# Two weight-split subtractions per step moved to VectorE in the first block, and the weight decode's low bits moved to ScalarE

## The chip, the cores and the metric

The kernel runs on one core of one Trainium2 chip. The metric is the device time of one execution in microseconds. A program starts each execution by itself; several executions of one kernel give a median.

Five engines work side by side, each on its own queue in order: TensorE (PE in the profile, its weight loads PEld), VectorE (DVE), ScalarE (ACT), GpSimd (POOL) and SyncE (SP), which here only starts transfers. Instructions on different engines wait for each other through semaphores.

## What is computed

An attention layer over chunks of 32 tokens with 8 memory keys, then a feed-forward layer, then a soft mixture of eight experts. Cut to what matters here:

```
x   = attention(q, k, v, mem_k, mem_v)      # 3072 tokens x 512
h   = x @ w_in                              # 512 -> 2048
g   = s * relu(h)**2 + b
x   = g @ w_out                             # 2048 -> 512
out = soft_moe(x, phi, w1, w2)
```

`w_in` and `w_out` arrive in device memory as 64-bit floats (the factor they are scaled with makes them so), 16 slices of 1,024 columns on 128 partitions.

## The kernel before, in words

**Blocks and steps.** The 3,072 tokens are 6 blocks of 512 (`NB`), and the feed-forward width is 16 slices of 128 (`NF`). One step `n` is one slice of one block: 96 steps in all. A step multiplies the block's `x` by the slice's `w_in` (`mm_h`, L269), makes `g` of the result (`make_g`, L275 to L278), and one step later multiplies `g` by the slice's `w_out` (`mm_y`, L289), which adds up in four PSUM banks. The steps of block 0 are n = 0 to 15; they are called the first block here.

**Three products for one.** Each operand is split into a high part, rounded to the fast matmul format, and a low part, the remainder. High times high, high times low and low times high are added, so a step has 12 matmuls in `mm_h` and 12 in `mm_y`. The split of the weights is made anew in every step: `split_wi` (L256 on ScalarE rounds, L257 on GpSimd subtracts) and `split_wo` (L261 on ScalarE, L262 on GpSimd). They write the tiles `wi0`, `wi1`, `wo0`, `wo1` in turn.

**Decoding the weights.** In the first block only, the 64-bit floats are turned into 32-bit ones, in 32 halves of 512 columns, two per step (`w_decode`). A half lies as 512 pairs of 32-bit words (low word, high word) in a staging tile (`sp0` to `sp6`, later also the `yt` and `y` tiles). Four instructions decode it: L246 on VectorE clamps the high words, L247 on ScalarE shifts the exponent, L248 on VectorE shifts the low words right by 29 bits, so that their top three bits are left, and L249 on VectorE puts high and low together into the tile `w`. When L249 has read a staging tile, SyncE may load the next half into it (`w_load`, L237).

**Background work.** While the steps of block j run, the attention of block j+1 is done between them: for each of 4 head pairs a `qk` task (L179 on PE; L185, L187 memsets, then the softmax L193 to L199 on VectorE with L195 on ScalarE), a `tr` task two steps later (PE transposes L205 of the softmax's result `ep`, copies L208 and L212), and a `pv` task (L219). The table `bg` sets the steps at which they stand.

**What sets the order.** For PE and SP the instructions stand in the order in which the program is written. For VectorE, ScalarE and GpSimd a scheduler of the framework orders them when the program is built; on the chip each queue is then worked off strictly in that order. Before the steps, a list of tokens (`START`) writes out the start: loads, the attention of block 0, the first decodes and splits.

Of the kernel before, what the change touches and what calls it, by code (L numbers as in the profile page):

```python
# [7 lines left out]
F32 = mybir.dt.float32  # L8
F32R = mybir.dt.float32r
U32 = mybir.dt.uint32  # L10
AF = mybir.ActivationFunctionType
ALU = mybir.AluOpType
AX = mybir.AxisListType
# [3 lines left out]
NF = 16  # L17
# [17 lines left out]
def tile_attention_moe_softmoe(  # L35
# [13 lines left out]
    pe, act, dve, pool, sp = nc.tensor, nc.scalar, nc.vector, nc.gpsimd, nc.sync  # L49
# [69 lines left out]
    def r32(ap):  # L119
        return ap.bitcast(F32R)  # L120
# [4 lines left out]
    def hl(t):  # L125
        return t.rearrange("p (a n) -> p a n", a=2)


    def qv(u):
        return Q[u % 2].rearrange("p (c h n) -> p c h n", h=2, c=CB)  # L130

    def qsv(u):
        return hl(RT[1])[:, u % 2].rearrange("p (c n) -> p c n", c=CB)
# [9 lines left out]
    def pbv(u):  # L143
        return PB[u % 2].rearrange("p (i a h z n) -> p i a h z n", i=4, a=2, h=2, z=2)
# [17 lines left out]
    def spread_q(u):  # L162
        t, src = qv(u), qsv(u)
        act.activation(out=t[0:64, :, 0, :], in_=src[0:64], func=AF.Copy)
        dve.tensor_copy(t[64:128, :, 1, :], src[64:128])
# [23 lines left out]
    def att_soft(u, b, last=None):  # L189
# [4 lines left out]
        dve.tensor_tensor(out=E, in0=S, in1=mx.unsqueeze(2).to_broadcast([P, 8, 64]), op=ALU.subtract)  # L194
        act.activation(out=E, in_=E, func=AF.Exp, scale=0.125)  # L195
        dve.tensor_reduce(out=sm, in_=E, axis=AX.X, op=ALU.add)  # L196
# [4 lines left out]
    def att_tr(u, b, fast=False):  # L201
# [5 lines left out]
        dst = pbv(u)  # L207
        act.activation(out=dst[0:64, :, :, :, 0, :], in_=src[0:64], func=AF.Copy)  # L208
        if fast:
            act.activation(out=dst[64:128, :, :, :, 1, :], in_=src[64:128], func=AF.Copy)  # L210
        else:
            dve.tensor_copy(dst[64:128, :, :, :, 1, :], src[64:128])  # L212

    def att_pv(u, b):
# [6 lines left out]
        xt = hl(X[j % 2][hp])  # L221
        act.activation(out=r32(xt[:, 0]), in_=b, func=AF.Copy)
        dve.tensor_tensor(out=r32(xt[:, 1]), in0=b, in1=xt[:, 0], op=ALU.subtract)
# [7 lines left out]
    def w_load(most=99):  # L231
        while stage_free and hnext[0] < len(halves) and most:
# [3 lines left out]
            t = stage_free.pop(0)  # L236
            sp.dma_start(out=t.bitcast(U32), in_=wd[f][:, 512 * h:512 * h + 512].bitcast(U32))  # L237
            stage_full.append((f, h, t))

    def w_decode():  # L240
        f, h, t = stage_full.pop(0)
        u = t.bitcast(U32).rearrange("p (n w) -> p n w", w=2)
        low, high = u[:, :, 0], u[:, :, 1]
        hv = t.rearrange("p (n w) -> p n w", w=2)[:, :, 1]
        dst = W[f][:, 512 * h:512 * h + 512].bitcast(U32)
        dve.tensor_scalar(out=hv, in0=hv, scalar1=-EXP_TOP, scalar2=EXP_TOP, op0=ALU.max, op1=ALU.min)  # L246
        act.activation(out=hv, in_=hv, func=AF.Prelu, scale=EXP_SHIFT, alpha=SIGN_SHIFT)  # L247
        dve.tensor_scalar(out=low, in0=low, scalar1=29, scalar2=None, op0=ALU.logical_shift_right)  # L248
        dve.scalar_tensor_tensor(out=dst, in0=high, scalar=3, in1=low, op0=ALU.logical_shift_left,  # L249
                                 op1=ALU.bitwise_or)  # L250
        stage_free.append(t)


    def split_wi(n):
        t, raw = hl(WI[n % 2]), W[n % NF][:, 0:512]
        act.activation(out=r32(t[:, 0]), in_=raw, func=AF.Copy)  # L256
        pool.tensor_tensor(out=r32(t[:, 1]), in0=raw, in1=t[:, 0], op=ALU.subtract)  # L257

    def split_wo(n):
        t, raw = hl(WO[n % 2]), W[n % NF][:, 512:1024]  # L260
        act.activation(out=r32(t[:, 0]), in_=raw, func=AF.Copy)  # L261
        pool.tensor_tensor(out=r32(t[:, 1]), in0=raw, in1=t[:, 0], op=ALU.subtract)  # L262

    def mm_h(n, kts):
        w = WI[n % 2].rearrange("p (a k c) -> p a k c", a=2, k=4)
# [221 lines left out]
    with tc.manual_schedule(engines={mybir.EngineType.PE, mybir.EngineType.SP}):  # L487
# [15 lines left out]
        for i in range(2):  # L503
            t = qv(i)
            pool.memset(t[0:64, :, 1, :], 0.0)
            pool.memset(t[64:128, :, 0, :], 0.0)
        for i in range(2):
            t = pbv(i)
# [5 lines left out]
        def s_qk(u):  # L514
# [15 lines left out]
            "T": lambda u: att_tr(u, sbank(), True),  # L530
            "P": lambda u: att_pv(u, sbank()),
            "D": lambda _: w_decode(),
            "I": split_wi,
            "O": split_wo,
            "H": lambda kt: mm_h(0, (kt,)),
            "y": lambda _: stage_free.extend(YT + Y),
# [5 lines left out]
        for n in range(NSTEP):  # L542
            j, f = divmod(n, NF)
            if n + 1 < NSTEP:
                split_wi(n + 1)
            split_wo(n)
            mm_h(n, (3,) if n == 0 else (0, 1, 2, 3))
            make_g(n)
            if n + 2 < NF:
                w_decode()  # L550
                w_decode()
                w_load()
# [261 lines left out]
```

## Time and profile before

| what | value |
|---|---|
| median of 3 executions | 710.28 us (709.08 to 711.67) |
| the profiled execution: its own time / its span from first to last instruction | 711.08 us / 709.2 us |
| mean granted TensorE clock | 0.984 of full speed |
| PE busy | 682.6 us, 96% of the span |
| PE weight loads busy | 536.4 us, 76% |
| DVE busy | 367.6 us, 52% |
| ACT busy | 338.2 us, 48% |
| POOL busy | 268.1 us, 38% |

The 1.9 us between own time and span lie outside the instructions. The shares are means over the whole span. Cut into 40 slices of 17.7 us, the profile has VectorE at 57999983 tenths in the first eight slices and at 2 to 7 tenths in nearly all the others, and PE at 7788979 in the first seven and at 9 (full) in every one after that. The start and the first block therefore have to be read apart from the rest: the steps of the first block run from about 39 us to about 140 us, and its last decode on VectorE ends at 114 us.

### The profile page before, as it was taken

The numbers are of one execution on the slowest core, as the hardware profiler recorded it, in microseconds if no ns is written. First come the engines' busy times: TensorE is split into PE (matmuls) and PEld (weight loads), VectorE is DVE, ScalarE is ACT, GpSimd is POOL, SyncE is SP. The second block draws the span as 40 slices with busy tenths as digits, with TensorE's granted clock in tenths as the row PEclk, the third lists the DMA queues.
The fourth block names the chain that finished last, engine by engine and source line by source line (L and its number), as shares of the span: only waits on it lengthen the run. The fifth ranks groups of instructions, "written<-read, shape, count | busy, mean of one in ns | idle before, by whom it ended". The sixth has DMA issues, their size and how long they took to land.

```text
span 709.2 us, 12315 instructions
## 1 busy us (share of the span) xinstructions
PE 682.6 (96%) x4961; PEld 536.4 (76%) x4961; DVE 367.6 (52%) x644; ACT 338.2 (48%) x596; POOL 268.1 (38%) x210
## 2 busy tenths in 40 slices
PE   7788979999999999999999999999999999999995
PEld 3577758888878888878888788888788888787353
DVE  5799998356445356545356535455544332223233
ACT  3555565445534455444455444445454544444332
POOL 4334555443434433344433443434334444441000
PEclk9899989999999999999999999999999999999998
DMA  8998622342022112202112202211113622538898
GB/s 321 344 407 299 199 107 90 117 181 90 9 82 91 30 60 90 73 18 90 36 55 90 90 1 90 90 32 59 61 39 119 259 90 90 204 93 267 230 292 340
DMA packets 47032, 94.38 MB, mean 133 GB/s; under 512 B 2944, under 2 KB 27520, under 8 KB 46976
## 3 DMA queue, kind: packets, MB, share of 16 engines
q1 hardware_dynamic: 46976, 93.60, 38.5%
q8 instruction: 39, 0.64, 0.4%
q14 instruction: 17, 0.14, 0.1%
HBM read 87.30 MB, written 6.29 MB: 132 GB/s over the span
## 4 chain that ended last, share of the span: by engine, by line
PE 85%; DVE 8%; DMA 3%; issue 2%; ACT 1%; POOL 0%; SPq 0%; ACTq 0%; DVEq 0%; POOLq 0%
PE bank L289 35%; PE bank L269 34%; PE bank L219 3%; PE bank L179 3%; PE bank L640 2%; PE bank L683 2%; DVE w L249 2%; PE bank L205 1%; DMA yt<-vd 1%; PE bank L333 1%; DMA k<-kd 1%; PE bank L311 1%; PE bank L349 1%; PE bank L709 1%; DMA out<-w 1%
## 5 line engine op out<-in xcount | busy, mean ns | idle before, releaser
L289 PE MATMUL bank<-g,wo 128*128 128x512 f32 x1152 | 287.7, 399 | 1.4 <-ACT g L277 1.1
L269 PE MATMUL bank<-x,wi 128*128 128x512 f32 x1152 | 279.2, 391 | 0.0
L269 PEld LDWEIGHTS bank<-x,wi 128*128 128x128 f32 x1152 | 217.3, 189 | 45.4
L289 PEld LDWEIGHTS bank<-g,wo 128*128 128x128 f32 x1152 | 212.7, 189 | 51.4 <-ACT wi L256 4.2
L262 POOL TENSOR_TENSOR wo<-w,wo 128x512 fp32r<-128x512 f32 x96 | 131.0, 1365 | 238.0 <-ACT wo L261 234.0
L276 DVE SCALAR_TENSOR_TENSOR rt<-bank,cons,rt 128x512 f32<-128x512 f32 x96 | 71.9, 749 | 236.4 <-ACT rt L275 236.0
L257 POOL TENSOR_TENSOR wi<-w,wi 128x512 fp32r<-128x512 f32 x96 | 127.0, 1323 | 122.5 <-ACT wi L256 120.9
L256 ACT ACTIVATE wi<-w 128x512 fp32r<-128x512 f32 x96 | 60.6, 632 | 149.7 <-PE bank L269 144.8
L277 ACT ACTIVATE g<-rt,cons 128x512 fp32r<-128x512 f32 x96 | 69.5, 724 | 44.4 <-DVE rt L276 42.7
L278 DVE SCALAR_TENSOR_TENSOR g<-rt,cons,g 128x512 fp32r<-128x512 f32 x96 | 73.4, 765 | 27.2 <-ACT g L277 24.5
L261 ACT ACTIVATE wo<-w 128x512 fp32r<-128x512 f32 x96 | 60.4, 629 | 53.5 <-PE bank L289 52.8
L275 ACT ACTIVATE rt<-bank 128x512 f32<-128x512 f32 x96 | 55.8, 582 | 7.2 <-PE bank L269 7.2
L195 ACT ACTIVATE ep<-ep 128x512 f32<-128x512 f32 x22 | 13.8, 628 | 32.6 <-DVE ep L194 32.6
L219 PEld LDWEIGHTS bank<-pb,v 128*64 128x64 f32 x704 | 22.3, 138 | 7.8 <-issue 7.0
L179 PE MATMUL bank<-k,q 128*64 128x64 f32 x704 | 25.5, 227 | 2.4 <-DMA k<-kd 2.4
L179 PEld LDWEIGHTS bank<-k,q 128*64 128x64 f32 x704 | 23.2, 142 | 6.0 <-issue 6.0
L219 PE MATMUL bank<-pb,v 128*64 128x64 f32 x704 | 25.3, 225 | 0.0
L247 ACT ACTIVATE sp<-sp 128x512 f32<-128x512 f32 x22 | 15.0, 686 | 14.6 <-DVE sp L246 14.4
L205 PE MATMUL bank<-cons,ep 128*128 128x128 f32 x88 | 13.9, 282 | 8.4 <-DVE ep L199 7.0
L249 DVE SCALAR_TENSOR_TENSOR w<-sp 128x512 uint32<-128x512 uint32 x22 | 19.8, 904 | 1.6 <-ACT sp L247 1.4
L205 PEld LDWEIGHTS bank<-cons,ep 128*128 128x128 f32 x88 | 10.8, 143 | 12.8 <-DVE ep L199 8.3
L196 DVE TENSOR_REDUCE ast<-ep 128x8 f32<-128x512 f32 x22 | 15.1, 685 | 10.0 <-ACT ep L195 9.9
(233 smaller groups left out, 519.3 us busy)
## 6 DMA issues: line engine op xcount, KB each, us to landing
sp<-wd SPq DMA_DIRECT2D x22, 512.0 KB, 7.6
k<-kd SPq DMA_DIRECT2D x22, 512.0 KB, 6.5
v<-vd SPq DMA_DIRECT2D x22, 512.0 KB, 3.7
q<-qd SPq DMA_DIRECT2D x20, 512.0 KB, 5.6
w<-e1d SPq DMA_DIRECT2D x10, 512.0 KB, 3.3
out<-w SPq DMA_DIRECT2D x9, 512.0 KB, 6.6
sp<-e1d SPq DMA_DIRECT2D x7, 512.0 KB, 7.3
sp<-e2d SPq DMA_DIRECT2D x7, 512.0 KB, 7.0
```

The source lines that it names most:

```text
L179: pe.matmul(S[64 * par:64 * par + 64, 2 * i + z, :], lhsT=qt[:, c].rearrange("p h n -> p (h n)"), rhs=kt[:, c, :], start=True, stop=True)
L219: pe.matmul(b[64 * h:64 * h + 64, 64 * m:64 * m + 64], lhsT=vt[:, m, h, :], rhs=pb[:, m // 2, m % 2, h].rearrange("p z n -> p (z n)"), sta ...
L256: act.activation(out=r32(t[:, 0]), in_=raw, func=AF.Copy)
L257: pool.tensor_tensor(out=r32(t[:, 1]), in0=raw, in1=t[:, 0], op=ALU.subtract)
L261: act.activation(out=r32(t[:, 0]), in_=raw, func=AF.Copy)
L262: pool.tensor_tensor(out=r32(t[:, 1]), in0=raw, in1=t[:, 0], op=ALU.subtract)
L269: pe.matmul(HB[n % 2], lhsT=r32(w[:, a, kt, :]), rhs=r32(x[:, b]), start=(kt == 0 and i == 0), stop=(kt == 3 and i == 2))
L275: act.activation(out=r, in_=HB[n % 2], func=AF.Relu, scale=1.0 / WSCALE ** 2)
L276: dve.scalar_tensor_tensor(out=t, in0=HB[n % 2], scalar=s_col, in1=r, op0=ALU.mult, op1=ALU.mult)
L277: act.activation(out=r32(g[:, 0]), in_=t, func=AF.Identity, bias=b_col)
L278: dve.scalar_tensor_tensor(out=r32(g[:, 1]), in0=t, scalar=b_col, in1=g[:, 0], op0=ALU.add, op1=ALU.subtract)
L289: pe.matmul(YB[dt], lhsT=r32(w[:, a, dt * 128:dt * 128 + 128]), rhs=r32(g[:, b]), start=(f == 0 and i == 0), stop=(f == NF - 1 and i == 2))
```

## The change

Two edits, both of which act in the first block only.

1. In `split_wi` and `split_wo` the subtraction goes to VectorE for n < 16 and stays on GpSimd for the other 80 steps: 32 instructions change engine.
2. In `w_decode` the VectorE shift by 29 bits of the low words is replaced by a ScalarE activation. It reads byte 3 of each 8-byte pair (the top byte of the low word, as an 8-bit integer), computes byte/32 - 31/64, and writes the result as a 32-bit integer into the low word; rounding to the nearest integer makes it the byte's top three bits. 32 instructions change engine.

```
+U8 = mybir.dt.uint8
...
         hv = t.rearrange("p (n w) -> p n w", w=2)[:, :, 1]
+        top = t.bitcast(U8).rearrange("p (n b) -> p n b", b=8)[:, :, 3]
         dst = W[f][:, 512 * h:512 * h + 512].bitcast(U32)
         dve.tensor_scalar(out=hv, in0=hv, scalar1=-EXP_TOP, scalar2=EXP_TOP, op0=ALU.max, op1=ALU.min)
         act.activation(out=hv, in_=hv, func=AF.Prelu, scale=EXP_SHIFT, alpha=SIGN_SHIFT)
-        dve.tensor_scalar(out=low, in0=low, scalar1=29, scalar2=None, op0=ALU.logical_shift_right)
+        act.activation(out=low, in_=top, func=AF.Copy, scale=1.0 / 32.0, bias=-31.0 / 64.0)
         dve.scalar_tensor_tensor(out=dst, in0=high, scalar=3, in1=low, op0=ALU.logical_shift_left,
                                  op1=ALU.bitwise_or)
...
     def split_wi(n):
         t, raw = hl(WI[n % 2]), W[n % NF][:, 0:512]
         act.activation(out=r32(t[:, 0]), in_=raw, func=AF.Copy)
-        pool.tensor_tensor(out=r32(t[:, 1]), in0=raw, in1=t[:, 0], op=ALU.subtract)
+        (dve if n < NF else pool).tensor_tensor(out=r32(t[:, 1]), in0=raw, in1=t[:, 0], op=ALU.subtract)
...
     def split_wo(n):
         t, raw = hl(WO[n % 2]), W[n % NF][:, 512:1024]
         act.activation(out=r32(t[:, 0]), in_=raw, func=AF.Copy)
-        pool.tensor_tensor(out=r32(t[:, 1]), in0=raw, in1=t[:, 0], op=ALU.subtract)
+        (dve if n < NF else pool).tensor_tensor(out=r32(t[:, 1]), in0=raw, in1=t[:, 0], op=ALU.subtract)
```

The new lines move the line numbers of the changed kernel: by one up to the decode, by two from its activation L247 on (L249 there) to the end. The order of PE and SP is the same in both kernels; that of VectorE, ScalarE and GpSimd is not. Two places matter below.

The first is VectorE's queue in steps 1 and 2, around the first softmax between the steps (`ast0` holds its statistics, `ep` its result; `rt` and `g` belong to `make_g`; `w2`, `w3` are decoded weights). Before:

```order
L276 SCALAR_TENSOR_TENSOR rt1_96<-bank5_144,cons_64,rt1_96 128x512
L194 TENSOR_TENSOR ep_109<-bank7_146,ast0_135 128x512
L248 TENSOR_SCALAR sp6_116<-sp6_116 128x512
L278 SCALAR_TENSOR_TENSOR g1_94<-rt1_96,cons_64,g1_94 128x512
L196 TENSOR_REDUCE ast0_135<-ep_109 128x8
L249 SCALAR_TENSOR_TENSOR w3_68<-sp6_116 128x512
L197 TENSOR_SCALAR ast0_135<-ast0_135 128x8
L246 TENSOR_SCALAR sp0_110<-sp0_110 128x512
L198 RECIPROCAL ast0_135<-ast0_135 128x8
L248 TENSOR_SCALAR sp0_110<-sp0_110 128x512
L199 TENSOR_TENSOR ep_109<-ep_109,ast0_135 128x512
```

The same place in the changed kernel:

```order
L278 SCALAR_TENSOR_TENSOR rt1_96<-bank5_144,cons_64,rt1_96 128x512
L195 TENSOR_TENSOR ep_109<-bank7_146,ast0_135 128x512
L248 TENSOR_SCALAR sp6_116<-sp6_116 128x512
L280 SCALAR_TENSOR_TENSOR g1_94<-rt1_96,cons_64,g1_94 128x512
L197 TENSOR_REDUCE ast0_135<-ep_109 128x8
L251 SCALAR_TENSOR_TENSOR w3_68<-sp6_116 128x512
L198 TENSOR_SCALAR ast0_135<-ast0_135 128x8
L248 TENSOR_SCALAR sp0_110<-sp0_110 128x512
L199 RECIPROCAL ast0_135<-ast0_135 128x8
L264 TENSOR_TENSOR wo0_83<-w2_67,wo0_83 128x512
L200 TENSOR_TENSOR ep_109<-ep_109,ast0_135 128x512
```

L248 here is the clamp (L246 before). The shifts of `sp6` and `sp0` are gone, the clamp of `sp6` has moved to behind L195, and the subtraction for `wo0` now stands between the reciprocal and the last multiplication of the softmax. Another subtraction, for `wi0`, stands three rows above the piece shown, just ahead of step 0's last `make_g` instruction.

The second place is ScalarE's queue around the third softmax between the steps, in step 7 and at the start of step 8. Before:

```order
L277 ACTIVATE g1_94<-rt1_96,cons_64 128x512
L261 ACTIVATE wo0_83<-w8_73 128x512
L247 ACTIVATE sp2_112<-sp2_112 128x512
L195 ACTIVATE ep_109<-ep_109 128x512
L247 ACTIVATE sp3_113<-sp3_113 128x512
L256 ACTIVATE wi0_81<-w10_75 128x512
L275 ACTIVATE rt0_95<-bank4_143 128x512
```

The same place in the changed kernel, where L250 is the new low-bit activation and L196 the softmax's exponential:

```order
L279 ACTIVATE g1_94<-rt1_96,cons_64 128x512
L249 ACTIVATE y1_108<-y1_108 128x512
L250 ACTIVATE sp3_113<-sp3_113 128x512
L250 ACTIVATE sp4_114<-sp4_114 128x512
L250 ACTIVATE sp5_115<-sp5_115 128x512
L263 ACTIVATE wo0_83<-w8_73 128x512
L250 ACTIVATE sp6_116<-sp6_116 128x512
L250 ACTIVATE sp0_110<-sp0_110 128x512
L196 ACTIVATE ep_109<-ep_109 128x512
L277 ACTIVATE rt0_95<-bank4_143 128x512
```

Five low-bit activations, each of which waits for nothing but the landing of its half, now stand ahead of the exponential and of the next `make_g`.

## Rows read from the trace of the kernel before

**Rows 1.** Stretches: busy us of each engine, granted clock, DMA share, GB/s

```profile
42.30:117.10 74.80, 66.37 (x445) 53.44 (x443) 73.29 (x129) 45.45 (x78) 36.45 (x21) 0.95 0.56 203
...
100.88:106.80 5.92, 5.92 (x16) 4.85 (x17) 5.86 (x12) 4.10 (x8) 5.22 (x2) 0.51 0.00 0
```

**Rows 2.** Timeline of PE: start, us, line, tiles [idle before <- releaser]

```profile
49.74 0.66 PE L205 MATMUL bank<-cons,ep 128*128 128x128 f32 x4 [1.82 <-DVE ep L199]
...
83.29 1.10 PE L179 MATMUL bank<-k,q 128*64 128x64 f32 x32
...
91.74 3.01 PE L289 MATMUL bank<-g,wo 128*128 128x512 f32 x12 [1.07 <-ACT g L277]
...
100.88 1.11 PE L205 MATMUL bank<-cons,ep 128*128 128x128 f32 x4 [3.40 <-DVE ep L199]
101.64 5.35 PE L289 MATMUL bank<-g,wo 128*128 128x512 f32 x12
...
117.12 3.02 PE L289 MATMUL bank<-g,wo 128*128 128x512 f32 x12
```

**Rows 3.** Waits, 35 to 120 us: total us, times, longest us

```profile
PE bank L205 <- DVE ep L199: 7.0, 3, 3.4
```

**Rows 4.** Timeline of DVE, first and third softmax between the steps

```profile
40.40 1.77 DVE L249 SCALAR_TENSOR_TENSOR w<-sp 128x512 uint32<-128x512 uint32 x1
...
46.66 1.60 DVE L249 SCALAR_TENSOR_TENSOR w<-sp 128x512 uint32<-128x512 uint32 x1
48.19 0.16 DVE L197 TENSOR_SCALAR ast<-ast 128x8 f32<-128x8 f32 x1
...
91.51 0.07 DVE L187 MEMSET bank<- 64x8 f32 x1
```

**Rows 5.** Timeline of POOL, two of the subtractions

```profile
46.43 1.28 POOL L262 TENSOR_TENSOR wo<-w,wo 128x512 fp32r<-128x512 f32 x1 [4.81 <-ACT wo L261]
...
101.58 4.55 POOL L262 TENSOR_TENSOR wo<-w,wo 128x512 fp32r<-128x512 f32 x1 [2.44 <-ACT wo L261]
```

**Rows 6.** Timeline of DVE, instructions directly behind each other

```profile
100.14 0.68 DVE L199 TENSOR_TENSOR ep<-ep,ast 128x512 f32<-128x512 f32 x1
100.74 0.68 DVE L249 SCALAR_TENSOR_TENSOR w<-sp 128x512 uint32<-128x512 uint32 x1
101.34 0.74 DVE L278 SCALAR_TENSOR_TENSOR g<-rt,cons,g 128x512 fp32r<-128x512 f32 x1
102.01 0.42 DVE L248 TENSOR_SCALAR sp<-sp 128x512 uint32<-128x512 uint32 x1
102.34 0.41 DVE L246 TENSOR_SCALAR sp<-sp 128x512 f32<-128x512 f32 x1
```

**Rows 7.** DVE by line and form, 42.3 to 117.1 us: busy us, mean ns | idle before

```profile
L249 DVE SCALAR_TENSOR_TENSOR w<-sp 128x512 uint32<-128x512 uint32 x16 | 14.6, 917 | 0.1
L278 DVE SCALAR_TENSOR_TENSOR g<-rt,cons,g 128x512 fp32r<-128x512 f32 x11 | 9.6, 874 | 0.0
...
L246 DVE TENSOR_SCALAR sp<-sp 128x512 f32<-128x512 f32 x16 | 8.0, 500 | 0.1
L248 DVE TENSOR_SCALAR sp<-sp 128x512 uint32<-128x512 uint32 x16 | 7.7, 483 | 0.1
L249 DVE SCALAR_TENSOR_TENSOR w<-yt 128x512 uint32<-128x512 uint32 x6 | 5.7, 942 | 0.0
L248 DVE TENSOR_SCALAR yt<-yt 128x512 uint32<-128x512 uint32 x6 | 3.6, 599 | 0.0
L246 DVE TENSOR_SCALAR y<-y 128x512 f32<-128x512 f32 x4 | 2.7, 685 | 0.0
L197 DVE TENSOR_SCALAR ast<-ast 128x8 f32<-128x8 f32 x3 | 2.7, 891 | 0.0
```

**Rows 8.** ACT by line and form, 42.3 to 117.1 us

```profile
L247 ACT ACTIVATE sp<-sp 128x512 f32<-128x512 f32 x16 | 11.0, 691 | 12.6 <-DVE sp L246 12.4
...
L256 ACT ACTIVATE wi<-w 128x512 fp32r<-128x512 f32 x11 | 7.0, 634 | 2.1 <-DVE ast L197 2.0
```

More of the change, by code (lines that the diff above doesn't have):

```diff
@@ L10 @@
 U32 = mybir.dt.uint32
+U8 = mybir.dt.uint8
 AF = mybir.ActivationFunctionType
@@ L244, in w_decode @@
         hv = t.rearrange("p (n w) -> p n w", w=2)[:, :, 1]
+        top = t.bitcast(U8).rearrange("p (n b) -> p n b", b=8)[:, :, 3]
         dst = W[f][:, 512 * h:512 * h + 512].bitcast(U32)
@@ L247, in w_decode @@
         act.activation(out=hv, in_=hv, func=AF.Prelu, scale=EXP_SHIFT, alpha=SIGN_SHIFT)
-        dve.tensor_scalar(out=low, in0=low, scalar1=29, scalar2=None, op0=ALU.logical_shift_right)
+        act.activation(out=low, in_=top, func=AF.Copy, scale=1.0 / 32.0, bias=-31.0 / 64.0)
         dve.scalar_tensor_tensor(out=dst, in0=high, scalar=3, in1=low, op0=ALU.logical_shift_left,
@@ L256, in split_wi @@
         act.activation(out=r32(t[:, 0]), in_=raw, func=AF.Copy)
-        pool.tensor_tensor(out=r32(t[:, 1]), in0=raw, in1=t[:, 0], op=ALU.subtract)
+        (dve if n < NF else pool).tensor_tensor(out=r32(t[:, 1]), in0=raw, in1=t[:, 0], op=ALU.subtract)
     def split_wo(n):
@@ L261, in split_wo @@
         act.activation(out=r32(t[:, 0]), in_=raw, func=AF.Copy)
-        pool.tensor_tensor(out=r32(t[:, 1]), in0=raw, in1=t[:, 0], op=ALU.subtract)
+        (dve if n < NF else pool).tensor_tensor(out=r32(t[:, 1]), in0=raw, in1=t[:, 0], op=ALU.subtract)
     def mm_h(n, kts):
```

## The prediction

> **What bounds the kernel now.** I read the busy time by stretches first, to find out where PE is not full; then PE's timeline there, for what it waits for; then VectorE's timeline and groups of instructions by line, for why what PE waits for is late. The stretch on which everything below is worked out runs from the first `mm_y` matmul to the eleventh, 42.3 to 117.1 us. In its 74.8 us VectorE is busy 73.3 us, with 129 instructions; ScalarE 45.45, GpSimd 36.45 [rows 1]. Outside it neither edit meets a full VectorE for long, and behind it PE is full.
>
> What PE loses in the stretch: three waits of PE's transposes for the last multiplication of a softmax, 7.0 us together [rows 3], of which the first is 1.82 and the third 3.40; one wait of 1.07 for `g`; and, behind the third wait, slow matmuls: four transposes in 1.11 us where 0.66 is usual, twelve `mm_y` matmuls in 5.35 where 3.02 is usual [rows 2], at a granted clock of 0.51, which is the lower level of 1.2 GHz [rows 1]. That is 7.0 + 1.07 + 0.45 + 2.33 = 10.9 us. PE itself needs 74.8 - 10.9 = 63.9 us for the stretch.
>
> Why the softmax is late: its scores left PE at 84.39 us (83.29 + 1.10), and VectorE took up the first instruction on them at 91.51 [rows 2, 4], 7 us later, because its queue was behind. VectorE was not only full, it was also held up. An L249 that takes 0.68 us otherwise [rows 6] took 1.60 when it started at 46.66, 0.23 us after a GpSimd subtraction of 1.28 us had started [rows 4, 5]. It went the other way too: the subtraction at 101.58, with VectorE's instructions back to back, took 4.55 us instead of 1.28 [rows 5, 6]. The two engines shut each other out.
>
> **The change on VectorE.** How much of its 73.3 us is being shut out? Mean against undisturbed time, by form [rows 6, 7]: L249 16 x (0.917 - 0.68) + 6 x (0.942 - 0.68) = 5.4; L278 11 x (0.874 - 0.74) = 1.5; L246 16 x (0.500 - 0.41) + 4 x (0.685 - 0.41) = 2.5; L248 16 x (0.483 - 0.42) + 6 x (0.599 - 0.42) = 2.1; L197, with 0.16 undisturbed [rows 4], 3 x (0.891 - 0.16) = 2.2. Sum 13.7 us. The 21 subtractions of the stretch (11 for `wi`, 10 for `wo`) thus cost VectorE 0.65 us each while GpSimd does them.
>
> - Edit 1 takes the 21 from GpSimd, which has nothing left that reads or writes at the same time: -13.7 us. It adds 21 instructions to VectorE. The trace has no such subtraction there. From below the price is that of an instruction with one input, 0.33 us from start to start (102.01 to 102.34); from above a held-up L249, 0.92 long, about 0.84 apart. The nearest row is L199: the same size, two inputs from SBUF, 0.60 to the next start [rows 6]. I take that: +12.6 us.
> - Edit 2 takes 26 shifts (16 + 6 and 4 on the `y` tiles) of 0.33 us: -8.6 us.
>
> VectorE then needs 73.3 - 13.7 + 12.6 - 8.6 = 63.6 us against PE's 63.9. So it is no longer behind, but it has nothing to spare either. Edit 1 alone would be worth 1.1 us of VectorE's time; most comes from edit 2. What edit 1 gives besides is that a subtraction no longer takes 4.55 us.
>
> A rule in the Trainium skill speaks against edit 1: its page "Perfetto Trace Analysis", section "Optimizing Scalar/DVE Operations", advises offloading work from a saturated DVE to Scalar or even GPSIMD, with the warning that between DVE and GPSIMD this might not help, since they share a port. By the first half alone the edit would add 12.6 us to the fullest engine; the measured 0.65 against 0.60 us per subtraction sides with the warning.
>
> **The change on ScalarE.** It gains 26 activations over 512 elements. The trace has none that reads bytes or writes integers. Nearest are L256 (packed in and out), 0.634 us, and L247, with the same spacing of 8 bytes, 0.691 [rows 8]; farther off lie VectorE's shift, 0.42 [rows 6], and GpSimd's pass, 1.28 [rows 5]. I take 0.66: 45.45 + 26 x 0.66 = 62.6 us, under PE's 63.9. With 0.42 it would be 56.4, with 1.28 it would be 78.7. So the cover is there, but it is thin.
>
> The Trainium skill's page "ScalarE: Activation LUTs", section "Rules for kernel authors", says to use VectorE rather than ScalarE for adds and multiplications, and its section on the table load gives 186 ns + 0.833 ns per element for an activation with immediate scale and bias. That makes an estimate of 0.61 us, or 61.3 us for ScalarE; the rows agree that ScalarE's pass is the dearer one, 0.66 against 0.42.
>
> **GpSimd, the DMA queue, PE's order.** GpSimd loses 32 instructions and keeps four multiplications in the start. PE and SyncE keep their order. Loads start when L249 frees a staging tile, so they come earlier with it; the DMA share of the stretch is 0.56 [rows 1], 42 us of transfers, which fit into 64. I cost this at nothing.
>
> **The sum.** All of the 10.9 us goes if no softmax is late. At the first one VectorE is hardly behind yet. There, two hold-ups go (1.77 - 0.68 and 1.60 - 0.68, together 2.0 us [rows 4]), and two shifts of the piece shown (0.7); two subtractions come ahead of the softmax's end (1.2). That is 1.5 us for a wait of 1.82, and the exponential on ScalarE lies in that chain as well; I leave half of the wait, 0.9 us. So 10.0 us are saved: 711.08 - 10.0 = 701.1 for the profiled execution. The median of the runs shown lies 0.80 below it, so **700.3 us**.
>
> **The rivals.**
> - *VectorE stays the bound.* If a subtraction takes 0.84 us, VectorE needs 63.6 + 21 x 0.24 = 68.6 us, 4.7 over PE, and 5.3 of the 10.0 are saved: 705.0. For: the two sums lie 0.3 us apart. Against: L199's own rows.
> - *ScalarE's order puts the wait back.* Five low-bit activations stand ahead of the third softmax's exponential in the changed queue, each waiting for a load. If a load is late there, the queue stands still and the softmax is late with it. With the third wait and its slow matmuls kept (3.40 + 0.45 + 2.33 = 6.2 us), 3.8 are saved: 706.5. Against: VectorE waited for nothing ahead of its 16 clamps L246 (0.1 us in all [rows 7]), so the halves now land before their turn.
> - *ScalarE becomes the bound, slower.* It gives back the whole stretch at (74.8 - 45.45) / 26 = 1.13 us per low-bit activation; at 1.28 the stretch grows to 78.7 us, +3.9: 714.2. For: no row has bytes or integers on ScalarE. Against: L247 with the same spacing needs 0.691.
> - *The change doesn't do what it says.* If the 13.7 us of stretching are not GpSimd's doing, VectorE needs 73.3 - 8.6 + 12.6 = 77.3 us, 2.5 more than the stretch: 712.8. Against: the pairs of rows above, in both directions.
> - *The loads cap it.* If halves don't land sooner, the time stays at about 710.3. Against: the DMA share of 0.56.
>
> **How the numbers follow.** Forecast 0.70, VectorE still the bound 0.10, ScalarE's order 0.10, loads 0.04, the two slower ones 0.06 together. A measurement of this kernel can tell about 0.3%, 2.1 us, from no change. The first three are faster by more than that, 0.90; the loads case is no change, 0.04; the rest is slower, 0.06. The range reaches from 697.1 (all 10.9 us; 1.2 us more, by which the lowest run shown lies under the median; and 1.1 us if the stretch also begins sooner by the hold-up at 40.40 [rows 4]) to 706.5, the dearest of the faster cases.
>
> **What would show it.** In the changed kernel's profile: VectorE's L251, L248 and L198 at their undisturbed 0.68, 0.42 and 0.16 us throughout; subtractions of about 0.68 us on VectorE; low-bit activations of 0.63 to 0.69 us; the memset that opens the third softmax within 1 or 2 us of the end of its scores on PE; no PE wait of over 2 us behind 42 us, and a granted clock of 1.00 from there on. I am wrong if ScalarE is the engine that PE waits for, if L250 takes over 0.8 us, or if VectorE is still at 99% with the waits at L205 in place.

## The result and the profile after

The changed kernel takes 700.57 us (median of 4 executions, 698.44 to 700.81) against 710.18 in the runs beside it; the ratio is 0.9857, with a 95% interval of 0.983 to 0.9883. The forecast was 700.3. The profiled execution took 700.81 us with a span of 698.9. The number was right; one step of its working was not, and it is the one that tells where the gain comes from.

Lines of the changed kernel: L251 is the old L249 (high and low put together), L248 the clamp, L259 and L264 the moved subtractions, L250 the new low-bit activation, L291 the `mm_y` matmuls, L206 the transposes that wait for the softmax.

The stretch from the first to the eleventh `mm_y` matmul group, in the columns of [rows 1]:

```profile
44.18:107.36 63.18, 62.67 (x445) 51.65 (x443) 62.33 (x122) 56.27 (x102) 0.00 (x0) 1.00 0.66 245
```

It is 63.18 us long instead of 74.80. VectorE is still busy nearly all the time, 62.33 us, ScalarE 56.27, GpSimd does nothing, and the granted clock is 1.00, the level of 2.4 GHz, throughout. PE's timeline of the stretch, which answers to [rows 2]:

```profile
44.18 2.88 PE L291 MATMUL bank<-g,wo 128*128 128x512 f32 x12
50.29 0.66 PE L206 MATMUL bank<-cons,ep 128*128 128x128 f32 x4 [0.51 <-DVE ep L200]
...
81.84 1.10 PE L180 MATMUL bank<-k,q 128*64 128x64 f32 x32
...
94.24 3.02 PE L291 MATMUL bank<-g,wo 128*128 128x512 f32 x12
...
107.36 3.02 PE L291 MATMUL bank<-g,wo 128*128 128x512 f32 x12
```

Of the three waits for a softmax, 7.0 us [rows 3], 0.51 us is left at the first. Behind the third softmax the twelve `mm_y` matmuls take 3.02 us instead of 5.35. Its scores leave PE at 82.94 us (81.84 + 1.10), and VectorE opens that softmax 2.3 us later, where it took 7 (1 or 2 had been forecast):

```profile
85.28 0.07 DVE L188 MEMSET bank<- 64x8 f32 x1
```

VectorE's instructions by line and form in the stretch (busy us, mean ns | idle before), against [rows 7]:

```profile
L251 DVE SCALAR_TENSOR_TENSOR w<-sp 128x512 uint32<-128x512 uint32 x16 | 10.9, 684 | 0.1
...
L259 DVE TENSOR_TENSOR wi<-w,wi 128x512 fp32r<-128x512 f32 x11 | 7.6, 689 | 0.1
L264 DVE TENSOR_TENSOR wo<-w,wo 128x512 fp32r<-128x512 f32 x10 | 6.8, 682 | 0.0
...
L198 DVE TENSOR_SCALAR ast<-ast 128x8 f32<-128x8 f32 x3 | 0.5, 165 | 0.0
```

None is stretched any more: 684 ns instead of 917, and 165 ns instead of 891 for the small one. The subtraction takes 0.69 us.

ScalarE, as in [rows 8]:

```profile
L249 ACT ACTIVATE sp<-sp 128x512 f32<-128x512 f32 x16 | 10.3, 669 | 2.4 <-DVE sp L248 2.4
L250 ACT ACTIVATE sp<-sp 128x512 uint32<-128x512 uint8 x15 | 9.3, 668 | 0.0
```

The low-bit activation takes 0.668 us, what the one beside it takes.

**What was given back.** The stretch begins at 44.18 us instead of 42.30, so 1.9 of its 11.6 us are lost ahead of it. In the kernel before, GpSimd multiplied the first softmax of the start, and PE's transposes followed, at these times (GpSimd's and PE's timeline):

```profile
14.72 1.04 POOL L199 TENSOR_TENSOR ep<-ep,ast 128x512 f32<-128x512 f32 x1 [5.59 <-DVE ast L198]
...
15.81 0.66 PE L205 MATMUL bank<-cons,ep 128*128 128x128 f32 x4 [1.17 <-POOL ep L199]
```

In the changed kernel, VectorE's timeline and PE's:

```profile
11.64 0.69 DVE L259 TENSOR_TENSOR wi<-w,wi 128x512 fp32r<-128x512 f32 x1
...
14.20 0.07 DVE L186 MEMSET bank<- 64x16 f32 x1 [0.81 <-PE bank L180]
14.30 0.69 DVE L197 TENSOR_REDUCE ast<-ep 128x8 f32<-128x512 f32 x1
...
17.83 0.65 PE L206 MATMUL bank<-cons,ep 128*128 128x128 f32 x4 [2.66 <-POOL ep L200]
```

The very first subtraction, `w_in` of step 0, has landed in the middle of the first softmax. With it the scheduler has put the memset of the second softmax, which waits for PE, ahead of the sum L197 of the first. In VectorE's queue before, that sum stood first. The first transposes come 2 us later in these two executions; how much of that is the order's doing is taken up below, under the start.

### The profile page after: what moved, and what is told of

Read it like the earlier page. It is cut to its first block, busy times and chain, and to the rows that moved or that the text cites. A ratio compares the mean times of both kernels' runs of the same rounds, so it can differ in the third digit from the quotient of the medians.

```text
span 698.9 us, 12246 instructions
## 1 busy us (share of the span) xinstructions
PE 679.8 (97%) x4961; PEld 535.0 (77%) x4961; DVE 357.2 (51%) x644; ACT 353.5 (51%) x628; POOL 217.1 (31%) x178
## 4 chain that ended last, share of the span: by engine, by line
PE 92%; DMA 4%; DVE 1%; ACT 1%; issue 0%; SPq 0%; POOL 0%; POOLq 0%; ACTq 0%
PE bank L291 38%; PE bank L271 37%; PE bank L220 4%; PE bank L180 3%; PE bank L642 2%; PE bank L685 2%; PE bank L206 1%; DMA out<-w 1%; DMA yt<-vd 1%; PE bank L335 1%; DMA k<-kd 1%; PE bank L313 1%; PE bank L351 1%; PE bank L503 1%; PE bank L711 1%; PE bank L389 0%
## 5 line engine op out<-in xcount | busy, mean ns | idle before, releaser
L291 PE MATMUL bank<-g,wo 128*128 128x512 f32 x1152 | 285.0, 396 | 0.0
L291 PEld LDWEIGHTS bank<-g,wo 128*128 128x128 f32 x1152 | 211.2, 188 | 48.8 <-ACT wi L258 4.2
L278 DVE SCALAR_TENSOR_TENSOR rt<-bank,cons,rt 128x512 f32<-128x512 f32 x96 | 72.0, 750 | 228.7 <-ACT rt L277 228.6
L264 POOL TENSOR_TENSOR wo<-w,wo 128x512 fp32r<-128x512 f32 x80 | 103.2, 1290 | 205.2 <-ACT wo L263 205.2
L259 POOL TENSOR_TENSOR wi<-w,wi 128x512 fp32r<-128x512 f32 x80 | 103.4, 1293 | 190.7 <-ACT wi L258 190.7
L280 DVE SCALAR_TENSOR_TENSOR g<-rt,cons,g 128x512 fp32r<-128x512 f32 x96 | 72.0, 750 | 27.3 <-ACT g L279 24.7
L196 ACT ACTIVATE ep<-ep 128x512 f32<-128x512 f32 x22 | 13.8, 628 | 31.3 <-DVE ep L195 31.3
L197 DVE TENSOR_REDUCE ast<-ep 128x8 f32<-128x512 f32 x22 | 15.1, 685 | 9.2 <-ACT ep L196 9.0
L223 ACT ACTIVATE x<-bank 128x512 fp32r<-128x512 f32 x24 | 14.3, 596 | 7.1 <-PE bank L220 4.6
L224 DVE TENSOR_TENSOR x<-bank,x 128x512 fp32r<-128x512 f32 x24 | 16.6, 691 | 0.7 <-ACT x L223 0.6
L194 DVE TENSOR_REDUCE ast<-bank 128x8 f32<-128x512 f32 x24 | 16.5, 687 | 0.4
L251 DVE SCALAR_TENSOR_TENSOR w<-sp 128x512 uint32<-128x512 uint32 x22 | 15.0, 685 | 2.8 <-ACT sp L249 2.6
```

Source lines behind the costliest of these rows:

```text
L259: (dve if n < NF else pool).tensor_tensor(out=r32(t[:, 1]), in0=raw, in1=t[:, 0], op=ALU.subtract)
L264: (dve if n < NF else pool).tensor_tensor(out=r32(t[:, 1]), in0=raw, in1=t[:, 0], op=ALU.subtract)
L278: dve.scalar_tensor_tensor(out=t, in0=HB[n % 2], scalar=s_col, in1=r, op0=ALU.mult, op1=ALU.mult)
L280: dve.scalar_tensor_tensor(out=r32(g[:, 1]), in0=t, scalar=b_col, in1=g[:, 0], op0=ALU.add, op1=ALU.subtract)
L291: pe.matmul(YB[dt], lhsT=r32(w[:, a, dt * 128:dt * 128 + 128]), rhs=r32(g[:, b]), start=(f == 0 and i == 0), stop=(f == NF - 1 and i == 2))
```

## The experiments

Twelve kernels, grouped by question. The stretch is always that from the first to the eleventh `mm_y`, in the columns of [rows 1]. The kernel before was run beside them; its medians there were 709.75 to 711.2 us.

### Each edit alone

Edit 1 without edit 2:

```
-        act.activation(out=low, in_=top, func=AF.Copy, scale=1.0 / 32.0, bias=-31.0 / 64.0)
+        dve.tensor_scalar(out=low, in0=low, scalar1=29, scalar2=None, op0=ALU.logical_shift_right)
```

> Edit 1 alone: the subtractions of the first block on VectorE, the shift by 29 bits still on VectorE. Theory A (VectorE's queue is the bound, and a sum of its instructions says how much): 73.3 - 13.7 + 12.6 = 72.2 us of VectorE in the stretch from the first to the eleventh w_out group of matmuls, against PE's 63.9, so most of the gain is missing: 707 to 710 us, VectorE at 99% and the waits of PE's transposes for the softmax still there, though every VectorE instruction takes its undisturbed time (L249 0.68, L197 0.16). Theory B (being shut out by GpSimd is the whole trouble): most of the gain comes with this edit alone, 700 to 704 us.

Measured: 700.39 us (698.12 to 700.93), ratio 0.9859 (0.9822 to 0.9896). The whole gain is there without edit 2. Its stretch, and the one wait of PE in it:

```profile
42.80:107.36 64.56, 62.66 (x445) 51.65 (x443) 64.00 (x131) 41.41 (x70) 0.00 (x0) 1.00 0.65 231
```
```profile
50.31 0.55 PE L205 MATMUL bank<-cons,ep 128*128 128x128 f32 x3 [1.91 <-DVE ep L199]
```

Edit 2 without edit 1:

```
-        (dve if n < NF else pool).tensor_tensor(out=r32(t[:, 1]), in0=raw, in1=t[:, 0], op=ALU.subtract)
+        pool.tensor_tensor(out=r32(t[:, 1]), in0=raw, in1=t[:, 0], op=ALU.subtract)
```

(in both splits)

> Edit 2 alone: the low bits on ScalarE, the subtractions still on GpSimd. Theory A: VectorE needs 73.3 - 8.6 = 64.7 us or a little more (it is still held up about 0.65 us by each of 21 subtractions) against PE's 63.9, so most of the gain is there: 700 to 704 us. Since the start keeps its old order of the first softmax, the stretch would begin at about 42.3 us and not at 44.2. Theory B: without edit 1 the hold-ups and the subtractions that GpSimd can't finish keep PE waiting: 705 to 709 us.

Measured: 710.69 us (708.26 to 711.88), ratio 1.0006 (0.9988 to 1.0023): nothing, and above both ranges. The stretch, PE's two waits for a softmax, and VectorE's hold-ups around the first of them:

```profile
41.59:117.75 76.16, 68.29 (x445) 55.66 (x443) 65.00 (x103) 58.02 (x103) 29.43 (x21) 0.91 0.56 206
```
```profile
50.51 1.12 PE L206 MATMUL bank<-cons,ep 128*128 128x128 f32 x4 [3.32 <-DVE ep L200]
...
101.45 1.11 PE L206 MATMUL bank<-cons,ep 128*128 128x128 f32 x4 [4.55 <-DVE ep L200]
```
```profile
45.29 1.21 DVE L248 TENSOR_SCALAR sp<-sp 128x512 f32<-128x512 f32 x1
...
48.20 1.66 DVE L251 SCALAR_TENSOR_TENSOR w<-sp 128x512 uint32<-128x512 uint32 x1
```

This is the most telling of the twelve. VectorE is busy 65.00 us instead of 73.29, 8.3 less, as edit 2 promised, and the stretch is no shorter: 76.16. VectorE is no longer full, and PE waits for it as before, 7.9 us for the softmax. Two instructions between the first softmax's start and end are still held up by GpSimd, by 0.8 us (1.21 - 0.42) and 1.0 (1.66 - 0.68).

### The start

Both edits, but the first subtraction left on GpSimd:

```
     def split_wi(n):
-        (dve if n < NF else pool).tensor_tensor(...)
+        (dve if 0 < n < NF else pool).tensor_tensor(...)
```

> Both edits, but the very first w_in subtraction (step 0) stays on GpSimd, which puts the first softmax of the start back into the order of the kernel before (sum of the exponentials ahead of the memset that waits for PE). Theory A (the changed kernel's stretch begins 1.9 us late because of that order): first transposes on PE at about 15.8 us and not 17.8, the stretch begins at about 42.3 us, 698 to 699.2 us in all, 0.2% to 0.4% under the changed kernel. Theory B (the transfers set the end of the start, whatever the order): the same as the changed kernel, 700 to 701 us.

Measured: 697.92 us (697.03 to 698.21), ratio 0.9832 (0.9804 to 0.9861). It is the fastest complete version of this study.

```profile
14.69 0.66 PE L206 MATMUL bank<-cons,ep 128*128 128x128 f32 x4 [1.53 <-POOL ep L200]
```
```profile
41.29:104.45 63.16, 62.66 (x446) 51.64 (x444) 62.31 (x122) 56.25 (x102) 0.00 (x0) 1.00 0.66 240
```

The first transposes come at 14.69 instead of 17.83 us, and the stretch is the same to 0.02 us, only 2.9 us earlier (44.18 - 41.29); the medians lie 2.65 us apart. In its queue L197 stands ahead of the memset again. So the place of that one subtraction did cost the start time, but not all of this difference is its doing. Between 8 and 13 us the granted clock was 0.66, a mean over both levels, in the profiled execution of the changed kernel and 1.00 in this one (the columns of [rows 1], the changed kernel first):

```profile
8.00:13.00 5.00, 4.61 (x38) 2.81 (x38) 2.51 (x6) 0.66 (x2) 0.00 (x0) 0.66 0.80 299
```
```profile
8.00:13.00 5.00, 5.00 (x70) 2.96 (x70) 3.45 (x9) 1.78 (x3) 0.78 (x1) 1.00 0.98 370
```

Both values occur with both orders, so the order can be priced at each. At 0.66 to 0.69 the first transposes come at 15.81 us in the kernel before and at 15.88 with edit 1 alone, which has its order of the first softmax, against 17.83 in the changed kernel: 2 us. At 1.00 they come at 14.69 here, against 15.81 with the changed order in a kernel that follows below, the one with the subtractions on VectorE in every block: 1.1 us.

### The price of the activation

Both edits, the low-bit activation issued twice:

```
+        act.activation(out=low, in_=top, func=AF.Copy, scale=1.0 / 32.0, bias=-31.0 / 64.0)
         act.activation(out=low, in_=top, func=AF.Copy, scale=1.0 / 32.0, bias=-31.0 / 64.0)
```

> Both edits, and every low-bit activation is issued twice (the first into the decoded weight's tile, which is overwritten after it). ScalarE was busy 56.3 us in the 63.2 us of the stretch in the changed kernel. Theory A (ScalarE's cover is thin): 26 more at 0.56 us from start to start make 70.9 us, ScalarE becomes the bound, the stretch grows by about 7.7 us: 706 to 710 us, with PE waiting for activations or for a softmax that is late. Theory B (ScalarE runs ahead and its queue has room): within 1.5 us of the changed kernel, 700 to 702 us.

Measured: 703.93 us (702.74 to 704.51), ratio 0.9917 (0.9887 to 0.9947), between the two.

```profile
44.56:110.88 66.32, 64.28 (x446) 52.92 (x444) 61.72 (x118) 65.43 (x120) 0.00 (x0) 0.97 0.64 234
```
```profile
52.21 1.04 PE L206 MATMUL bank<-cons,ep 128*128 128x128 f32 x4 [2.04 <-DVE ep L200]
52.91 4.32 PE L292 MATMUL bank<-g,wo 128*128 128x512 f32 x12
```

With twice the work ScalarE is the full engine, 65.43 of 66.32 us. It costs 3.4 us over the changed kernel. The stretch is 3.1 us longer, nearly all of it at the first softmax: PE waits 2.04 us instead of 0.51, and the twelve `mm_y` matmuls behind the wait (L292 here) take 4.32 us, where 3.02 is usual. ScalarE's cover in the changed kernel is real, and thin.

### Being held up, taken by itself

Edit 1 does two things: it takes GpSimd's subtractions away from beside VectorE, and it leads the scheduler to another VectorE queue. To have the first alone, the kernel before without the 32 subtractions:

```
     def split_wi(n):
-        pool.tensor_tensor(out=r32(t[:, 1]), in0=raw, in1=t[:, 0], op=ALU.subtract)
+        if n >= NF:
+            pool.tensor_tensor(out=r32(t[:, 1]), in0=raw, in1=t[:, 0], op=ALU.subtract)
...
+        for t in WI + WO:
+            pool.memset(hl(t)[:, 1], 0.0)
```

(the same in `split_wo`)

> The kernel before, without the 32 subtractions on GpSimd in the first block. It leaves out the low part of the split weights there (it is set to zero once, in the start). VectorE's queue in the stretch is that of the kernel before, instruction for instruction. Theory A (being held up by GpSimd is what makes VectorE late): its 73.3 us in the stretch fall by 13.7 to 59.6, under PE's 63.9, the waits for the softmax go, and the time is 699 to 702 us. Theory B (the softmax is late because halves are decoded ahead of it in VectorE's queue, more of them than the steps need): the queue is the same, so most of the waits stay, and the time is 706 to 711 us.

Measured: 698.11 us (696.65 to 699.31), ratio 0.9825 (0.98 to 0.9849). Theory A's number, with VectorE's queue unchanged.

```profile
43.26:106.17 62.91, 62.67 (x445) 51.64 (x443) 58.99 (x126) 46.02 (x78) 0.00 (x0) 1.00 0.64 240
```
```profile
49.10 0.66 PE L205 MATMUL bank<-cons,ep 128*128 128x128 f32 x4 [0.24 <-DVE ep L199]
```
```profile
L249 DVE SCALAR_TENSOR_TENSOR w<-sp 128x512 uint32<-128x512 uint32 x16 | 10.9, 686 | 0.1
...
L246 DVE TENSOR_SCALAR sp<-sp 128x512 f32<-128x512 f32 x15 | 6.4, 423 | 0.1
```

VectorE does the same 26 halves in the same order and needs 58.99 us instead of 73.29, 14.3 less. Three instructions fewer lie in this stretch, 126 against 129: one second half of `g`, one clamp and one memset, about 1.1 us. So some 13.2 us were being held up, where the rows had given 13.7. With that alone gone the stretch is as short as with the whole change.

Half of edit 1, only the `w_out` subtractions on VectorE:

```
     def split_wi(n):
-        (dve if n < NF else pool).tensor_tensor(...)
+        pool.tensor_tensor(...)
```

(from the kernel with edit 1 alone)

> Half of edit 1: only the w_out subtractions of the first block move to VectorE, the w_in subtractions stay on GpSimd, the shift stays on VectorE. Theory A (each GpSimd subtraction holds VectorE up, and the waits follow from that): about half of the gain, 703 to 707 us. Theory B (the waits depend on which instruction of a softmax is hit, a few hits decide): anything between 699 and 711, with PE's waits at the places where a GpSimd subtraction ran beside a softmax's instructions.

Measured: 706.43 us (704.71 to 708.44), ratio 0.9951 (0.9933 to 0.9969).

```profile
41.65:110.61 68.96, 64.49 (x446) 52.72 (x444) 67.96 (x127) 40.86 (x71) 16.16 (x10) 0.98 0.61 216
```

About a third of the gain, inside theory A's range; theory B's range holds it too, so this run doesn't tell them apart. With 10 of the subtractions still on GpSimd the stretch, 68.96 us, lies about halfway between 74.80 and 64.56; a further wait for a softmax, 2.07 us at 124 us, follows behind it.

### VectorE's order, taken by itself

The kernel before, GpSimd and shift untouched, with VectorE's queue in the first block in the order in which the program is written (a second guard around the steps, with VectorE among its engines):

```
         for n in range(NSTEP):
+            with (tc.manual_schedule(engines={mybir.EngineType.PE, mybir.EngineType.SP, mybir.EngineType.DVE}) if n < NF
+                  else ExitStack()):
...
```

> The kernel before, with the 32 subtractions on GpSimd and the shift on VectorE as before; only that VectorE's queue in the steps of the first block stands in the order in which the program is written: two halves decoded per step and no decode between the instructions of a softmax. Theory A (being held up): GpSimd's subtractions still hold VectorE up, some 5 halves fewer in the stretch take about 6 us off it, the softmax chain itself is still stretched, and the time is 705 to 711 us. Theory B (what stands ahead of the softmax in the queue): the waits for the softmax go although the holding up stays, and the time is 699 to 703 us.

Measured: 727.56 us (726.96 to 728.74), ratio 1.0242 (1.0218 to 1.0266), outside both ranges.

```profile
39.84:119.18 79.34, 67.33 (x446) 53.89 (x444) 64.26 (x109) 40.54 (x69) 26.79 (x20) 0.94 0.55 195
```
```profile
81.79 1.33 DVE L249 SCALAR_TENSOR_TENSOR w<-sp 128x512 uint32<-128x512 uint32 x1 [0.58 <-ACT sp L247]
...
85.42 0.75 DVE L278 SCALAR_TENSOR_TENSOR g<-rt,cons,g 128x512 fp32r<-128x512 f32 x1 [0.79 <-ACT g L277]
```

VectorE is busy only 64.26 of 79.34 us: in the written order it stands still at 12 of its 20 L249 and at 6 L278, 10.7 us together, until ScalarE has done the instruction before, since nothing lies between the two. The experiment swapped one fault of the order for another and doesn't tell the theories apart. The same guard with edit 2:

> Edit 2 alone (low bits on ScalarE, subtractions on GpSimd), with VectorE's queue in the steps of the first block in the written order. Theory B: as with the written order and the shift on VectorE, 698 to 703 us, so that edit 2 alone gained nothing only because of the order that the scheduler gave it. Theory A: GpSimd's holding up is still there, as in edit 2 alone: 707 to 711 us.

Measured: 729.03 us (726.75 to 729.68), ratio 1.0255 (1.0229 to 1.0281). The same objection holds.

### How full VectorE really is

Each subtraction issued twice, with edit 1 alone and with both edits:

```
+        for _ in range(2 if n < NF else 1):
             (dve if n < NF else pool).tensor_tensor(out=r32(t[:, 1]), in0=raw, in1=t[:, 0], op=ALU.subtract)
```

> Edit 1 alone, with each of the 32 subtractions of the first block issued twice on VectorE. With edit 1 alone VectorE was busy 64.0 of the 64.6 us of the stretch, with 20 subtractions in it. Theory A (VectorE is at its edge there, what it gets more the stretch becomes longer): 20 x 0.60 = 12 us more, 708 to 714 us. Theory B (VectorE is only busy because it works ahead on halves that are not due yet, it gives those up and PE hardly waits): 700 to 704 us.

Measured: 719.42 us (718.79 to 720.33), ratio 1.0131 (1.0106 to 1.0157).

> Both edits, with each of the 32 subtractions of the first block issued twice on VectorE. If edit 2 gives VectorE a reserve that is used when VectorE is too full (Theory A of edit 1 with the subtractions twice), 22 shifts of 0.33 us, 7 us, lie between the two: 701 to 706 us against 708 to 714. If VectorE has a reserve anyway (Theory B), both lie within 2 us of each other, 700 to 704 us.

Measured: 714.35 us (711.8 to 715.31), ratio 1.0056 (1.003 to 1.0082). The two stretches, edit 1 first:

```profile
42.68:118.73 76.05, 65.57 (x446) 52.42 (x444) 74.60 (x148) 41.00 (x70) 0.00 (x0) 0.98 0.58 204
```
```profile
43.67:117.07 73.40, 65.45 (x446) 52.20 (x444) 68.39 (x128) 54.55 (x95) 0.00 (x0) 0.98 0.58 205
```

The first stretch grows by 11.5 us, from 64.56 to 76.05, what theory A had worked out as 12; the time grows by 19, more than its range, because two more waits follow behind the stretch (3.15 us for a softmax at 133 us, with slow matmuls behind it, and 1.16 for a copy at 142). So with edit 1 VectorE is at its edge. Edit 2 is worth 5.1 us there, 2.7 of them in the stretch. That is not 7, and 714.35 lies above both of that kernel's ranges, but it is worth something. VectorE has a new wait with it, 3.5 us for ScalarE ahead of the second half of `g` (VectorE by line, both edits with the subtractions issued twice):

```profile
L282 DVE SCALAR_TENSOR_TENSOR g<-rt,cons,g 128x512 fp32r<-128x512 f32 x10 | 7.4, 745 | 3.6 <-ACT g L281 3.5
```

### Without edit 2, and in every block

Edit 1 alone, with the first subtraction on GpSimd as in the fastest version:

> Edit 1 alone, with the very first subtraction (w_in of step 0) left on GpSimd. If edit 2 gives nothing at all, this is as fast as both edits with that first subtraction on GpSimd, 697.9 us: 697 to 700.5. If edit 2 is worth something once VectorE is free of GpSimd, it is over 700.5.

Measured: 699.57 us (699.04 to 699.91), ratio 0.9849 (0.9825 to 0.9872). By the bounds set beforehand that is the case in which edit 2 gives nothing, but they were too wide to show a gain of 1 or 2 us.

```profile
41.67:106.23 64.56, 62.65 (x445) 51.64 (x443) 63.63 (x130) 41.40 (x70) 0.00 (x0) 1.00 0.66 231
```

Against the fastest version, edit 2 is worth 1.40 us of the stretch (64.56 - 63.16), and the medians lie 1.65 us apart. The two ran in different groups and their ratios' intervals overlap, so the time alone doesn't prove it; but edit 1 alone and both edits show the same 1.38 us between their stretches (64.56 - 63.18), both times at the first softmax.

Both edits, with the subtractions on VectorE in all six blocks (the condition dropped):

> Both edits, and the subtractions on VectorE in all six blocks instead of the first alone. Behind the first block PE is full and VectorE half idle, so every theory expects the time of the changed kernel within 0.3%, 698.5 to 702.5 us; if GpSimd's subtractions held up something on PE's path in the later blocks too, it would be under 698.

Measured: 699.56 us (698.86 to 700.49), ratio 0.9847 (0.9824 to 0.987), the changed kernel's time within what can be told. Behind the first block it doesn't matter which engine subtracts.

## Why the prediction was right, and where it was not

**What bounds the kernel** was read rightly: three softmaxes late on VectorE, 10.9 us of PE's time. The changed stretch is 62.67 us of PE and one wait of 0.51; PE's own need had been put at 63.9, 1.2 too high; 0.3 of that is a wait for `g` at 86.75 us that was not counted.

**The size of the holding up** was right: 13.7 us from the means, about 13.2 by the run without the subtractions. That was the step on which the forecast rested, and it could be had from the trace of the kernel before alone.

**The step that failed** is "Edit 1 alone would be worth 1.1 us of VectorE's time; most comes from edit 2". Edit 1 alone gives 10 us (1.41% of 709.95), edit 2 alone nothing. The sum 73.3 - 13.7 + 12.6 treated VectorE's work in the stretch as fixed. It isn't: VectorE decodes ahead. The ten steps need 20 halves; the kernel before did 26 in the stretch [rows 7]. With the subtractions in VectorE's queue the scheduler spread the decodes. With edit 1 alone VectorE's halves in the stretch are, by line and form:

```profile
L249 DVE SCALAR_TENSOR_TENSOR w<-sp 128x512 uint32<-128x512 uint32 x13 | 8.9, 688 | 0.1
...
L249 DVE SCALAR_TENSOR_TENSOR w<-yt 128x512 uint32<-128x512 uint32 x4 | 2.8, 691 | 0.0
L249 DVE SCALAR_TENSOR_TENSOR w<-y 128x512 uint32<-128x512 uint32 x4 | 2.8, 688 | 0.0
```

That makes 21, and the last of the block begins at 124.3 us instead of 113.6. The run without the subtractions gives the base: 58.99 us with 26 halves. 20 subtractions at 0.60 are 12.0, five halves fewer at 1.27 (0.34 + 0.33 + 0.60 from start to start) are 6.3: 64.7 us, against 64.00 measured. With 26 halves the same sum gives 71, over PE's 62.7 (an estimate; it wasn't tried). By this sum edit 1 pays by two things at once: the holding up goes, and 6 us of work that was not due moves behind the stretch. The run without the subtractions shows that the first alone shortens the stretch; that the second is needed once VectorE does the subtractions itself is worked out, not shown.

**Why edit 2 alone gives nothing** has the other half of it. It takes 8.3 us of VectorE's work, and PE's waits stay at 7.9 us in two places. Part of what was freed went into halves that are not due: from the first `mm_y` to the third softmax's transposes VectorE works on 24 halves, the first of them under way at the start, where it was 20 in the kernel before. Another part, 2.8 us there, went into waits of L251 for ScalarE, and the hold-ups stayed inside the softmax's own chain. Those are rows, not runs: the two experiments that were to hold the order fixed with GpSimd at work failed, so how the rest divides between the order and the hold-ups in that kernel is open.

**VectorE with both edits**: 62.33 us, forecast 63.6, and by the same base 58.99 + 21 x 0.60 - 26 x 0.33 = 63.0. It does 26 halves again, six more than the steps need. "It has nothing to spare" was too dark for the changed kernel and right for edit 1 alone, as the doubled subtractions show.

**ScalarE**: 56.27 us, forecast 62.6. One low-bit activation takes 0.67 us, forecast 0.66; but directly behind another one starts 0.55 to 0.56 after it, so the 25 in the stretch are 13.9 us and not 16.5. The older activations stand closer together as well: 45.45 us over 78 instructions were 0.58 each, 56.27 over 102 are 0.55. So ScalarE's busy time grew by 10.8 us only. The rival of ScalarE becoming the bound needed 1.13 us; twice the activation brought 3.4 us, not a reversal.

**The first wait**: 0.9 us were left for it, 0.51 stayed. Here edit 2 does have its use: 1.91 without it.

**The start** was missed. Nothing was costed ahead of the stretch, and the range only allowed for a gain there. The order of VectorE's first 20 instructions had changed, and reading it would have shown the memset that waits for PE ahead of the first softmax's sum. In the profiled executions 1.9 us of the stretch's 11.6 were lost there, and it is why the changed kernel is no faster than edit 1 alone, whose profiled execution had the same clock in the start: edit 2 gains 1.4 us in the stretch, and the stretch begins 1.4 us later (44.18 against 42.80).

So where 10.0 us were forecast, the profiled execution saved 10.3 (711.08 - 700.81), from 11.6 us in the stretch, 1.9 lost ahead of it and 0.6 won behind it. Two misses nearly cancelled, and that the time came out so close is luck in part.

**The rivals.** That the stretching is not GpSimd's doing (712.8) is refuted by the run without the subtractions. VectorE as the bound (705.0) would have needed a subtraction of 0.84 us; it takes 0.60 to the next start. A late load ahead of the exponential and loads that cap the stretch did not show: the DMA share rose from 0.56 to 0.66.

The Trainium skill's page "Perfetto Trace Analysis", section "Optimizing Scalar/DVE Operations", advises offloading from a saturated DVE and warns that GPSIMD might not help because of a shared port. The runs side with the warning: a subtraction on GpSimd cost VectorE about 0.63 us (13.2 over 21), one of its own costs it 0.60.

## What to carry to other kernels

Before moving work off a full engine, compare the mean duration of each of its instructions with its undisturbed one: what it loses to a neighbour (here 13 of 73 us) isn't in the instruction count, and can be more than the work that the neighbour takes. A busy share of 99% doesn't say that all of it is due; where a scheduler lets an engine run ahead, count the pieces that the stretch needs, or a sum of costs will put the gain on the wrong edit. And read the changed order at the program's start as closely as in the stretch that pays: one moved subtraction cost 1 to 2 us there.

## What was not expected of the hardware

- The holding up hits a small instruction as hard as a large one: VectorE's 128x8 instruction took 0.891 us in the mean beside GpSimd's subtractions and 0.165 without them, and a large one went from 0.68 to 1.6 to 1.8. It works in the other direction too, 4.55 us for a GpSimd subtraction of 1.28 [rows 5].
- Not every instruction of VectorE is held up. In the kernel before, those that were (L246, L248, L249, L278, L197) read and write SBUF alone. Those that read PSUM (`bank` in the rows) kept their time beside a subtraction, as L223 does here, with L278 held up behind it:

```profile
60.19 1.73 POOL L257 TENSOR_TENSOR wi<-w,wi 128x512 fp32r<-128x512 f32 x1 [2.69 <-ACT wi L256]
```
```profile
60.69 0.68 DVE L223 TENSOR_TENSOR x<-bank,x 128x512 fp32r<-128x512 f32 x1
61.29 1.18 DVE L278 SCALAR_TENSOR_TENSOR g<-rt,cons,g 128x512 fp32r<-128x512 f32 x1
```

  And the subtraction of 4.55 us ended 1.24 us, about its undisturbed time, after VectorE had come to L276 at 104.89 us, which reads PSUM.
- ScalarE reads bytes at a spacing of 8 and writes 32-bit integers at the price of its other activations on 512 elements: 0.668 us against 0.669.
